# Seven block products for pairs of chunks at the end of a fused attention and feed-forward kernel, and zero products in planned pauses

## The chip, the cores and the metric

The kernel runs on one core of a Trainium2 chip. Each core has a matrix engine (PE, with its weight loads listed apart as PEld), a vector engine (DVE), a scalar engine (ACT), a general engine (POOL) and a queue engine that issues transfers (SP). They work at the same time and wait for one another by semaphores. The metric is the device time of one execution in microseconds (us); the median of several runs is compared.

## The reference

A linear attention is computed for 8 batches of 8 heads with 576 tokens and a head width of 64; its result, laid out as 4608 tokens by 512, goes through a feed-forward layer without bias.

```python
def phi(x):
    proj = np.einsum('bhsd,df->bhsf', x, w_phi)
    proj = proj - np.max(np.abs(proj), axis=-1, keepdims=True)
    return np.concatenate([np.exp(proj), np.exp(-proj)], axis=-1)
q_p, k_p = phi(q), phi(k)
kv = np.einsum('bhsf,bhsd->bhfd', k_p, v)
z = np.sum(k_p, axis=2)
num = np.einsum('bhsf,bhfd->bhsd', q_p, kv)
den = np.einsum('bhsf,bhf->bhs', q_p, z)[..., None] + 1e-06
x = (num / den)          # as 4608 x 512
h = x @ w_in             # 512 x 2048
r = np.maximum(h, 0.0)
out = (r * r) @ w_out    # 2048 x 512
```

## The kernel before

**Attention.** The 64 heads are handled as 32 pairs of heads (`p`). The first six pairs go through `early`, the others through `visit` (L847) and `late` (L936). One visit is a block of PE work: it starts the keys of pair i+1 (L588) and the queries of pair i (L856), forms keys times values of pair i (L644, L649) and the numerators of pair i-1 (L876). `late` holds what DVE, ACT and POOL do for a pair between two visits: maxima over partitions, two exponentials, the denominators. `tokens` then divides and writes the result of a pair into a ring of fp16 pairs (high part and remainder, L829 and L832), which holds six chunks of 256 tokens; its second half, `ring1`, is allocated when the weights are ready.

**Feed-forward.** `moe(c, f, w_done)` handles chunk `c` (18 chunks of 256 tokens) and block `f` (8 blocks of 256 hidden columns): 144 groups in all. `gemm1` (L1026) multiplies 4 slices of 128 of the 512 inputs, for each of two halves of 128 columns, in three products of fp16 parts (high by high, high by low, low by high): 24 matmuls of 256 columns into the PSUM tile `ph`. ACT applies Relu (L1035) and squares twice (L1039, L1041), DVE takes the remainder `gl` (L306), and `gemm2` (L1058) multiplies the squares by the output weights, again in three products: 12 matmuls of 512 columns into two `po` tiles, which gather over the 8 blocks and are then scaled and stored (`store`, L1076 and L1087).

**Order.** All work is entered in a planner (`P.add`) with an assumed duration, the operations that it follows, the tiles that it uses, and a rank. `order` runs a list scheduler over five queues by these numbers and the instructions are issued in the order that comes out, so each engine's order is fixed before the program runs. An operation of a lower rank goes first; on PE an operation of another array mode must be lower by `STAY` = 6. Pair `p` has ranks around 4.5 p, a visit i has rank 4.5 i + 1.3, and group n = 8 c + f of the feed-forward has rank `LEAD` + n = 36 + n. Its evictions have ranks lower by 1000, so they go ahead of all else on their engines. Ranks between -50 and 70 are replaced by a table found by an earlier search (`RANKS`, read by `improve`).

**PSUM.** The attention holds the tiles `pp` (two banks), `pn`, `pv` and `pz`; the feed-forward holds `ph` (one bank) and `po` (two). The four attention tiles have one buffer each, and their users are chained one after another.

**Start.** Eight products of zeros (`warm`, L419) run before the first load has landed. The weights are loaded, split in two parts and scaled by powers of two (`power`, with the tops `TOP_W` and `TOP_X`) beside the first six pairs.

Of the kernel before, what the change touches and what calls it, by code (L numbers as in the profile page):

```python
# [247 lines left out]
class Tiles:  # L248
# [10 lines left out]
    def __getitem__(self, n):  # L259
# [33 lines left out]
def tile_kernel(ctx, tc, qp, kp, vp, w_phi, w_in, w_out, out):  # L293
# [711 lines left out]

    chunk_done = {}

    def moe(c, f, w_done):
        n = c * NFP + f
        m, bank = LEAD + n, n + BANKS  # L1010
        half, c0 = divmod(c * T % RING, HR)
        po = [("po", 2 * BANKS + 2 * c + i) for i in range(2)]

        after = list(w_done[f, True])
        if f == 0:
            for p in range(NPAIR):
                after += [o for t0, t1, o in ring_of[p] if t0 < c * T + T and t1 > c * T]

        def gemm1():
            ph = ph_[bank]  # L1020
            for j in range(2):
                ff = 2 * f + j
                k = 0
                for t in range(KT):
                    for (w, x) in ((0, 0), (0, 1), (1, 0)):
                        PE.matmul(out=ph[:, j, :], lhsT=win[w][:, t, 128 * ff:128 * ff + 128],  # L1026
                                  rhs=ring[half][x][:, t, c0:c0 + T], start=k == 0, stop=k == 3 * KT - 1)
# [7 lines left out]
        o = P.add("ACT", act_us(512, 1), lambda: A.activation(  # L1035
            out=r_[n], in_=ph_[bank], func=AF.Relu, scale=cw[:, f, 0:1]), [g1], [("ph", bank), ("r", n)], Q,
                  other=[("DVE", 0.70, lambda: V.tensor_scalar(out=r_[n], in0=ph_[bank], scalar1=cw[:, f, 0:1], scalar2=0.0,
                                                               op0=ALU.mult, op1=ALU.max), None)])
        sq = P.add("ACT", act_us(512), lambda: A.activation(out=gh_[n], in_=r_[n], func=AF.Square),  # L1039
                   [o], [("r", n), ("gh", n)], Q)  # L1040
        o = P.add("ACT", act_us(512), lambda: A.activation(out=r_[n], in_=r_[n], func=AF.Square),  # L1041
                  [sq], [("r", n)], Q, other=[("DVE", 0.70, lambda: V.tensor_tensor(
                      out=r_[n], in0=r_[n], in1=r_[n], op=ALU.mult), 4.0)])
        o = P.add("DVE", 0.70, lambda: sub(V, gl_[n], r_[n], gh_[n].bitcast(F32)),
                  [o, sq], [("r", n), ("gh", n), ("gl", n)], Q, lock=4.0)


        def gemm2():
            upper = lambda x: x.bitcast(BF16).rearrange("p j (c w) -> p j c w", w=2)[:, :, :, 1]
            low, near = wout[f][1:]  # L1050
            parts = [(s, i) for s in range(3) for i in range(2)]
            if n == NCH * NFP - 1:
                parts = [(s, i) for i in range(2) for s in range(3)]
            for s, i in parts:
                g, w = ((gh_[n], highs[f]), (upper(gh_[n]), low), (gl_[n], near))[s]
                for j in range(2):
                    ff = 2 * f + j
                    PE.matmul(out=po_[po[i][1]], lhsT=g[:, j, 128 * i:128 * i + 128], rhs=w[:, j, :],  # L1058
                              start=(ff == 0 and s == 0), stop=(ff == 2 * NFP - 1 and s == 2))

        g2 = P.add("PE", 2.69, gemm2, [o] + list(w_done[f, False]),
                   [("gh", n), ("gl", n)] + po, m + 1.5)
        if f:
            g2.after.append(last2[0])
        last2[0] = g2
        if f == NFP - 1:
            for i in range(2):
                store(c, i, po[i], g2, Q)

    def store(c, i, po, g2, Q):  # L1070
        tt = 2 * c + i
# [11 lines left out]
        for E, x in ways:  # L1083
            n = x.stop - x.start
            o = P.add(*(("DVE", dve_us(n) + 0.11) if E is V else ("ACT", out_us(n) + 0.09)), lambda E=E, x=x: scaled(E, x),
                      [g2] + [scales] * (E is A), [po, ("o", tt)], Q)
            P.add("SP", 0.38, lambda x=x: SP.dma_start(out[128 * tt:128 * tt + 128, x], o_[tt][:, x]), [o], [("o", tt)], Q,  # L1087
                  land=1.8, xfer=0.7)

    last2 = [None]  # L1090

# [31 lines left out]
    for p in range(NPAIR):  # L1123
# [8 lines left out]
        if p == EARLY:  # L1132
# [5 lines left out]
    last_cc = cc[:, 2 * NCH - 2:2 * NCH]  # L1138
    scales = P.add("DVE", 0.2, lambda: V.tensor_tensor(out=cc2, in0=last_cc, in1=last_cc, op=ALU.mult),
                   [scale_of[B - 1]], [], PER_PAIR * NPAIR, lock=4.0)  # L1140
    for c in range(NCH):
        for f in range(NFP):
            moe(c, f, w_done)
    pool_next.after += pool_prep
    for op in P.ops:
        op.after = [x for a in op.after for x in (chunk_done[a[1]] if isinstance(a, tuple) else [a])]
    P.close()
    with tc.manual_schedule():
        for op in P.improve():
# [29 lines left out]


# [31 lines left out]
```

## Time and profile before

| | |
|---|---|
| median of 3 runs | 1044.22 us (1042.35 to 1044.98) |
| the profiled execution | 1042.14 us |
| its span, first to last instruction | 1040.4 us |
| PE busy | 1021.0 us, 98% |
| DVE busy | 735.0 us, 71% |
| ACT busy | 639.6 us, 61% |
| POOL busy | 169.0 us, 16% |
| mean granted PE clock | 0.998 |

The busy time of PE contains the overlap of pipelined matmuls, so it doesn't tell by itself how much of it is needed. The span has a start in which transfers and the preparation of weights go on, a long middle in which visits and feed-forward groups alternate, and an end with feed-forward groups alone.

### The profile page before, as it was taken

The page shows a single profiled execution, that of the slowest core. Times are in us where ns is not written, and L with a number is a line of the kernel's source. Part 1 is how long each engine was busy: PE and PEld are TensorE (multiplying, and loading weights), DVE is VectorE, ACT ScalarE, POOL GpSimd, SP SyncE. Part 2 cuts the span into 40 slices and gives each one's busy share as a digit, 9 for nine tenths or more (in the row PEclk, how much of TensorE's full clock was granted, in tenths as well). Part 3 has the DMA queues.
Part 4 walks back from the last instruction along what each step waited for, and adds up shares of the span by engine and source line. Part 5 has one row for each costly group of instructions (what it writes and reads, how often), then busy time and mean ns, then how long its engine had stood idle before and what let it go on. Part 6 is the DMA issues. An engine that isn't in the chain of part 4 may idle for free.

```text
span 1040.4 us, 19694 instructions
## 1 busy us (share of the span) xinstructions
PE 1021.0 (98%) x7874; PEld 701.0 (67%) x7874; DVE 735.0 (71%) x1525; ACT 639.6 (61%) x1118; POOL 169.0 (16%) x87
## 2 busy tenths in 40 slices
PE   8879999999999999999999999999999999999998
PEld 6546676676666766766766766676766666777775
DVE  6889788998877888889778787778787845111111
ACT  7988786667656666676666666566665635333333
POOL 2334231111111111121011111101111101000000
PEclk9999999999999999999999999999999999999999
DMA  9744322222212222222121221211121101000000
GB/s 358 271 158 140 134 67 58 79 58 58 78 59 78 58 65 67 79 61 76 31 65 47 76 60 58 73 28 57 45 66 34 44 17 38 1 22 21 1 21 21
DMA packets 66144, 73.49 MB, mean 71 GB/s; under 512 B 35204, under 2 KB 44036, under 8 KB 64004
## 3 DMA queue, kind: packets, MB, share of 16 engines
q1 hardware_dynamic: 66052, 72.22, 21.7%
q8 instruction: 62, 1.02, 0.4%
q14 instruction: 30, 0.25, 0.1%
HBM read 59.18 MB, written 12.99 MB: 69 GB/s over the span
## 4 chain that ended last, share of the span: by engine, by line
PE 94%; ACT 2%; DMA 2%; DVE 1%; SPq 0%; issue 0%; ACTq 0%
PE po L1058 37%; PE ph L1026 36%; PE pz L644 4%; PE pn L876 3%; PE pn L856 3%; PE pp L588 2%; PE pv L876 2%; DMA k<-in_kp_dram 2%; PE pz L649 1%; PE pz L864 1%; PE pv L644 1%; PE pz L594 1%; PE pn L758 0%; PE pn L775 0%; PE pp L739 0%; PE pv L677 0%
## 5 line engine op out<-in xcount | busy, mean ns | idle before, releaser
L1026 PE MATMUL ph<-ring,win 128*128 128x256 f16 x3456 | 401.0, 273 | 0.0
L1026 PEld LDWEIGHTS <-win 128*128 128x128 f16 x3456 | 336.6, 98 | 71.7 <-issue 6.7
L1035 ACT ACTIVATE r<-ph,cw 128x512 f32<-128x512 f32 x144 | 98.9, 687 | 262.1 <-PE ph L1026 261.1
L306 DVE TENSOR_TENSOR gl<-r,gh 128x512 bf16<-128x512 f32 x144 | 102.2, 709 | 193.7 <-ACT r L1041 192.9
L960 POOL PARTITION_ALL_REDUCE mx<-pt x52 | 119.8, 2303 | 604.2 <-ACT pt L310 557.5
L1058 PE MATMUL po<-wh,gh 128*128 128x512 f32 x576 | 170.3, 416 | 0.0
L1058 PE MATMUL po<-wl,gh 128*128 128x512 bf16 x576 | 149.6, 382 | 0.0
L1058 PE MATMUL po<-wl,gl 128*128 128x512 bf16 x576 | 148.0, 379 | 0.0
L1058 PEld LDWEIGHTS po<-wh,gh 128*128 128x128 f32 x576 | 97.8, 189 | 19.8 <-issue 4.7
L1058 PEld LDWEIGHTS <-gl 128*128 128x128 bf16 x576 | 56.3, 98 | 68.0
L1039 ACT ACTIVATE gh<-r 128x512 fp32r<-128x512 f32 x144 | 90.7, 630 | 6.8 <-PE po L1058 2.4
L1058 PEld LDWEIGHTS <-gh 128*128 128x128 bf16 x576 | 44.7, 98 | 73.3 <-issue 39.7
L1041 ACT ACTIVATE r<-r 128x512 f32<-128x512 f32 x144 | 90.7, 630 | 4.6
L610 ACT ACTIVATE e<-e 128x512 f32<-128x512 f32 x64 | 40.0, 626 | 35.7 <-DVE e L607 35.5
L604 DVE TENSOR_REDUCE km<-pp 128x4 f32<-128x512 f32 x54 | 36.6, 684 | 30.1 <-PE pp L588 30.0
L626 DVE TENSOR_TENSOR ez<-e 128x512 f32<-128x512 f32 x52 | 45.8, 880 | 5.1 <-ACT e L612 4.6
L644 PE MATMUL pz<-e,v 128*64 128x256 f32 x416 | 49.3, 379 | 0.0
L306 DVE TENSOR_TENSOR qe<-pt,mx 128x576 f32<-128x576 f32 x52 | 39.2, 753 | 10.0 <-POOL mx L960 9.8
L974 DVE SCALAR_TENSOR_TENSOR pt<-qe,zc,pt 128x576 f32<-128x576 f32 x52 | 41.7, 815 | 5.7 <-ACT pt L972 5.0
L972 ACT ACTIVATE pt<-qe,zc 128x576 f32<-128x576 f32 x52 | 40.1, 774 | 4.4 <-ACT qe L967 0.4
L612 ACT ACTIVATE e<-e 128x512 f32<-128x512 f32 x64 | 40.2, 628 | 1.4
L978 DVE STREAM_TRANSPOSE yt<-pt 128x576 f32<-128x576 f32 x52 | 40.3, 774 | 0.8
(205 smaller groups left out, 1257.2 us busy)
## 6 DMA issues: line engine op xcount, KB each, us to landing
v<-in_vp_dram SPq DMA_DIRECT2D x32, 320.0 KB
k<-in_kp_dram SPq DMA_DIRECT2D x32, 288.0 KB
q<-in_qp_dram SPq DMA_DIRECT2D x32, 288.0 KB
rb<-rd SPq DMA_DIRECT2D x64, 144.0 KB
out_dram<-o SPq DMA_DIRECT2D x34, 256.0 KB
td<-kvs SPq DMA_DIRECT2D x26, 128.0 KB
kz<-td SPq DMA_DIRECT2D x104, 32.0 KB
raw0i<-in_w_in_dram SPq DMA_DIRECT2D x1, 1024.0 KB
```

What stands on the lines that cost most here:

```text
L306: eng.tensor_tensor(out=out_, in0=a, in1=b_, op=ALU.subtract)
L626: o = P.add("DVE", dve_us(512), lambda n=n: V.tensor_tensor(out=ez_[n].rearrange("p t x -> p (t x)"), in0=e_[n][:, 0:2].rearrange("p t s f ...
L644: PE.matmul(out=to[64 * h:64 * h + 64, 0:256], lhsT=v_[p][:, t, h, :], rhs=e_[2 * p + h][:, t].rearrange("p s f -> p (s f)"), start=t == 0 ...
L876: PE.matmul(out=to[64 * h:64 * h + 64, :], lhsT=kz_[n][:, 128 * s_ + 64 * h:128 * s_ + 64 * h + 64], rhs=qe_[2 * n + h].rearrange("p (s x) ...
L960: o = P.add("POOL", par_us(S), lambda n=n, h=h: G.partition_all_reduce(mx_[n], pt_[p][:, h, :], channels=128, reduce_op=bass_isa.ReduceOp. ...
L974: o = P.add("DVE", 0.82, lambda h=h, qe=qe, y=y: V.scalar_tensor_tensor(out=y(), in0=qe(1), scalar=zc_[p][:, 2 * h + 1:2 * h + 2], in1=y() ...
L978: o = P.add("DVE", dve_us(S), lambda n=n, y=y: V.transpose(yt_["y", n - 2 * EARLY], y()), [o], [("pt", p), ("yt", ("y", n - 2 * EARLY))], ...
L1026: PE.matmul(out=ph[:, j, :], lhsT=win[w][:, t, 128 * ff:128 * ff + 128], rhs=ring[half][x][:, t, c0:c0 + T], start=k == 0, stop=k == 3 * K ...
L1035: o = P.add("ACT", act_us(512, 1), lambda: A.activation(out=r_[n], in_=ph_[bank], func=AF.Relu, scale=cw[:, f, 0:1]), [g1], [("ph", bank), ...
L1039: sq = P.add("ACT", act_us(512), lambda: A.activation(out=gh_[n], in_=r_[n], func=AF.Square), [o], [("r", n), ("gh", n)], Q)
L1041: o = P.add("ACT", act_us(512), lambda: A.activation(out=r_[n], in_=r_[n], func=AF.Square), [sq], [("r", n)], Q, other=[("DVE", 0.70, lamb ...
L1058: PE.matmul(out=po_[po[i][1]], lhsT=g[:, j, 128 * i:128 * i + 128], rhs=w[:, j, :], start=(ff == 0 and s == 0), stop=(ff == 2 * NFP - 1 an ...
```

## The change

The last four chunks (14 to 17) are handled as two pairs of chunks. For a pair of chunks and one block `f`, the first product is seen as a 2 by 2 block product: the weights as two halves of the columns by two halves of the inputs, the tokens as two halves of the inputs by two chunks. Seven products of blocks (`product`, six matmuls of 256 columns each) take the place of eight, so a pair and a block take 42 matmuls in place of 48. They need sums of blocks. Those of the weights (`add_w`, once for each `f`) and of the tokens (`add_x`, twice for each pair of chunks) are formed beforehand, mostly on DVE, in the new single tile `tm`, split in two fp16 parts and kept in tiles that the attention has left. The products go to `pz`, `pp` and `ph`; four DVE operations and one copy combine them, and the values go on through Relu, squares and `gemm2` as before. The results of the second chunk of a pair gather in `pn` and `pv`. Since sums of four values must stay in fp16's range, the tops of the powers of two are 2^-12 in place of 2^-14.

The ranks of the feed-forward are spread by `STEP` = 1.09; the table `RANKS` is another one, found for these ranks. Last, the planned order is searched for pauses of PE of over 0.7 us before 125 us; where an attention tile of PSUM is free in the plan, products of zeros into it are put there, as many of 0.214 us as fill 0.6 of the pause.

```diff
-TOP_W = 2.0 ** -14
-TOP_X = 2.0 ** -14
+TOP_W = 2.0 ** -12
+TOP_X = 2.0 ** -12
+STEP = 1.09
+FILL_TO = 125.0
+PAIRED = 14
+TAIL = LEAD + (STEP - 1.0) * PAIRED * NFP
...
+    tm_ = tiles(None, "tm", [128, 1024], F32, 1)
...
     def moe(c, f, w_done):
         n = c * NFP + f
-        m, bank = LEAD + n, n + BANKS
+        m, bank = LEAD + STEP * n, n + BANKS
...
+    def combine(fill, sums, use, halves, after, rank):
+        n = len(parts_w) + len(parts_x)
+        tm = lambda: tm_[n]
+        o = P.add("DVE", 1.3, fill, after + [ring1] + exps[NPAIR - 2], [("tm", n)], rank, lock=4.0)
+        o = P.add("DVE", 1.7, sums, [o], [("tm", n)], rank, lock=4.0)
+        hi = P.add("ACT", 1.06, lambda: A.activation(out=halves(0), in_=tm(), func=AF.Copy), [o], [("tm", n)] + use, rank,
+                   other=[("DVE", 0.64, lambda: V.tensor_copy(out=halves(0), in_=tm()), 4.0)])
+        return P.add("DVE", 1.28, lambda: sub(V, halves(1), tm(), halves(0)), [hi], [("tm", n)] + use, rank, lock=4.0)
...
+    def add_w(f, rank):
...
+            V.tensor_tensor(out=tm_[n].rearrange("p (t c) -> p t c", t=KT), in0=win[0][:, :, cs], in1=win[1][:, :, cs], op=ALU.add)
...
+            V.tensor_tensor(out=a22, in0=a21, in1=a22, op=ALU.add)
+            sub(V, a21, a11, a21)
+            sub(V, a11, a22, a11)
+            sub(V, a12, a12, a11)
...
+    def pair(c, f):
+        n = c * NFP + 2 * f
+        m = TAIL + n
+        Q = m - 1000.0
...
+        def product(to, l, r_):
+            fl, *al = left[l]
+            fr, *ar = right[r_]
+            n = 0
+            for k in range(2):
+                for x, y in ((0, 0), (0, 1), (1, 0)):
+                    PE.matmul(out=to, lhsT=fl(x, *al)(k), rhs=fr(y, *ar)(k), start=n == 0, stop=n == 5)
+                    n += 1
...
+        after = list(w_done[f, True]) + [w_ready] + x_ready + in_pair.get("pe", [])
+        if f == 0:
+            after += ready(c) + ready(c + 1)
+        reads = w_use + x_use
+        p1 = P.add("PE", 1.97, one, after, [px, pu] + reads, m)
+        p2 = P.add("PE", 2.62, two, [p1], [px, py] + reads, m + 0.01)
...
+        first, other = copy(T, lambda: r()[:, 2, :], lambda: pz_["w", g][:, 0:T])
+        o = P.add(*first, [p1] + old, [pu, rt], Q, other=[other])
+        u = P.add("DVE", dve_us(512), lambda: plus(r()[:, 0:2, :], X(0), wide(r()[:, 2, :])), [o], [px, rt], Q)
+        v = P.add("DVE", dve_us(512), lambda: plus(W(), X(1), wide(r()[:, 1, :])), [p2, u], [px, uv, rt], Q)
+        c22 = P.add("DVE", dve_us(T), lambda: plus(r()[:, 3, :], X(1)[:, 1, :], W()[:, 0, :]), [v], [px, uv, rt], Q)
+        c2 = P.add("DVE", dve_us(512), lambda: plus(r()[:, 1:3, :], Y(), W()), [v], [py, uv, rt], Q)
+        c3 = [P.add("ACT", act_us(512, 1), lambda i=i: A.activation(
+            out=r()[:, 2 * i:2 * i + 2, :], in_=r()[:, 2 * i:2 * i + 2, :], func=AF.Relu, scale=cw[:, f, 0:1]),
+            [c2, c22], [rt], Q + 0.1 * i) for i in range(2)]
+        for i in range(2):
+            done.append(squares(n + i, lambda i=i: r()[:, 2 * i:2 * i + 2, :], [c3[i]], [rt], Q + 0.1 * i))
+            second(n + i, c + i, f, done[i], m + 2.5 + i, po[i])
...
-    for c in range(NCH):
+    for c in range(PAIRED):
         for f in range(NFP):
             moe(c, f, w_done)
...
+    for c in range(PAIRED, NCH, 2):
+        first = TAIL + c * NFP - (6.0 if c == PAIRED else 8.0)
+        for f in range(3 if c == PAIRED else 0):
+            add_w(f, first + 0.5 * f)
+        for i in range(2):
+            add_x(c, i, [next(keep), next(keep)], first + 2.0 + 0.5 * i)
+        for f in range(3, NFP if c == PAIRED else 0):
+            add_w(f, first + 0.5 + f)
+        for f in range(NFP):
+            pair(c, f)
...
+    def zeros(tag, n, count):
+        to = {"pp": pp_, "pn": pn_, "pv": pv_, "pz": pz_}[tag]["fill", n]
+        for _ in range(count):
+            PE.matmul(out=to[:, 0, :] if tag == "pp" else to, lhsT=warmer[:, 0:128], rhs=warmer, start=True, stop=True)
...
+        if op.eng == "PE":
+            if last and last.end < FILL_TO and op.start - last.end > 0.7:
+                gaps.append((last.end, op.start))
+            last = op
+    fills = []
+    for n, (t0, t1) in enumerate(gaps):
+        free = [tag for tag in ("pp", "pv", "pz", "pn")
+                if all(y + 0.2 <= t0 or x >= t1 for (k, _), (x, y) in held.items() if k == tag)]
+        if free:
+            fills.append((t0, len(P.ops), lambda tag=free[0], n=n, count=int(0.6 * (t1 - t0) / 0.214): zeros(tag, n, count)))
```

More of the change, by code (lines that the diff above doesn't have):

```diff
@@ L264, in __getitem__, with shaped @@
         return self.made[n]
+    def shaped(self, n, shape, dtype):
+        assert n not in self.made and (self.first is None or n == self.first + len(self.made)), (self.tag, n)
+        self.made[n] = self.pool.tile(shape, dtype, name=f"{self.tag}_{len(self.made)}", tag=self.tag, bufs=self.n)
+        return self.made[n]
 def act_us(n, pointers=0):
@@ L1006, in tile_kernel, with ready, at_ring @@
     chunk_done = {}
+    def ready(c, rows=range(NP)):
+        return [o for p in range(NPAIR) if p % NP in rows for t0, t1, o in ring_of[p] if t0 < c * T + T and t1 > c * T]
+    def at_ring(c, x, rows):
+        half, c0 = divmod(c * T % RING, HR)
+        return ring[half][x][:, rows, c0:c0 + T]
     def moe(c, f, w_done):
         n = c * NFP + f
-        m, bank = LEAD + n, n + BANKS
-        half, c0 = divmod(c * T % RING, HR)
-        po = [("po", 2 * BANKS + 2 * c + i) for i in range(2)]
+        m, bank = LEAD + STEP * n, n + BANKS
         after = list(w_done[f, True])
         if f == 0:
-            for p in range(NPAIR):
-                after += [o for t0, t1, o in ring_of[p] if t0 < c * T + T and t1 > c * T]
+            after += ready(c)
         def gemm1():
@@ L1026, in gemm1 @@
                         PE.matmul(out=ph[:, j, :], lhsT=win[w][:, t, 128 * ff:128 * ff + 128],
-                                  rhs=ring[half][x][:, t, c0:c0 + T], start=k == 0, stop=k == 3 * KT - 1)
+                                  rhs=at_ring(c, x, t), start=k == 0, stop=k == 3 * KT - 1)
                         k += 1
@@ L1038, in moe, with squares, second @@
                                                                op0=ALU.mult, op1=ALU.max), None)])
[L1039 to L1045, printed above, removed]
+        g = squares(n, lambda: r_[n], [o], [("r", n)], Q)
+        second(n, c, f, g, m + 1.5, [("po", 2 * BANKS + 2 * c + i) for i in range(2)])
+    def squares(n, r, after, use, Q):
+        sq = P.add("ACT", act_us(512), lambda: A.activation(out=gh_[n], in_=r(), func=AF.Square),
+                   after, use + [("gh", n)], Q)
+        o = P.add("ACT", act_us(512), lambda: A.activation(out=r(), in_=r(), func=AF.Square),
+                  [sq], use, Q, other=[("DVE", 0.70, lambda: V.tensor_tensor(
+                      out=r(), in0=r(), in1=r(), op=ALU.mult), 4.0)])
+        return P.add("DVE", 0.70, lambda: sub(V, gl_[n], r(), gh_[n].bitcast(F32)),
+                     [o, sq], use + [("gh", n), ("gl", n)], Q, lock=4.0)
+    def second(n, c, f, g, rank, po):
+        bank = lambda i: {"po": po_, "pn": pn_, "pv": pv_}[po[i][0]][po[i][1]]
         def gemm2():
@@ L1051, in gemm2 @@
             parts = [(s, i) for s in range(3) for i in range(2)]
-            if n == NCH * NFP - 1:
+            if c >= NCH - 2 and f == NFP - 1:
                 parts = [(s, i) for i in range(2) for s in range(3)]
             for s, i in parts:
-                g, w = ((gh_[n], highs[f]), (upper(gh_[n]), low), (gl_[n], near))[s]
+                x, w = ((gh_[n], highs[f]), (upper(gh_[n]), low), (gl_[n], near))[s]
                 for j in range(2):
                     ff = 2 * f + j
-                    PE.matmul(out=po_[po[i][1]], lhsT=g[:, j, 128 * i:128 * i + 128], rhs=w[:, j, :],
+                    PE.matmul(out=bank(i), lhsT=x[:, j, 128 * i:128 * i + 128], rhs=w[:, j, :],
                               start=(ff == 0 and s == 0), stop=(ff == 2 * NFP - 1 and s == 2))
-        g2 = P.add("PE", 2.69, gemm2, [o] + list(w_done[f, False]),
-                   [("gh", n), ("gl", n)] + po, m + 1.5)
-        if f:
+        g2 = P.add("PE", 2.69, gemm2, [g] + list(w_done[f, False]), [("gh", n), ("gl", n)] + po, rank)
+        if last2[0]:
             g2.after.append(last2[0])
@@ L1085, in store, with take @@
             o = P.add(*(("DVE", dve_us(n) + 0.11) if E is V else ("ACT", out_us(n) + 0.09)), lambda E=E, x=x: scaled(E, x),
-                      [g2] + [scales] * (E is A), [po, ("o", tt)], Q)
+                      [g2] + [scales] * (E is A), [use, ("o", tt)], Q)
             P.add("SP", 0.38, lambda x=x: SP.dma_start(out[128 * tt:128 * tt + 128, x], o_[tt][:, x]), [o], [("o", tt)], Q,
                   land=1.8, xfer=0.7)
+    parts_w, parts_x, in_pair = {}, {}, {}
+    def take(use, shape, dtype, box):
+        if use not in box:
+            box[use] = {"e": e_, "qe": qe_, "pt": pt_, "mx": mx_, "n": n_, "rb": rb_, "v": v_, "k": k_, "q": q_, "r": r_}[use[0]].shaped(
+                use[1], shape, dtype)
+        return box[use]
@@ new lines, in add_x, with fill, sums @@
+    def add_x(c, rows, use, rank):
+        n = len(parts_w) + len(parts_x)
+        box = {}
+        halves = lambda x: take(use[x], [128, 1024], F16, box)
+        grid = lambda x: x.rearrange("p (h c t) -> p h c t", h=2, c=2)
+        def fill():
+            for i in range(2):
+                V.tensor_tensor(out=grid(tm_[n])[:, :, i, :], in0=at_ring(c + i, 0, slice(rows, KT, 2)),
+                                in1=at_ring(c + i, 1, slice(rows, KT, 2)), op=ALU.add)
+        def sums():
+            x = grid(tm_[n])
+            b11, b12, b21, b22 = x[:, 0, 0, :], x[:, 0, 1, :], x[:, 1, 0, :], x[:, 1, 1, :]
+            sub(V, b11, b12, b11)
+            sub(V, b12, b22, b12)
+            sub(V, b22, b22, b11)
+            sub(V, b21, b21, b22)
+        o = combine(fill, sums, use, halves, [o for i in range(2) for o in ready(c + i, (rows, rows + 2))], rank)
+        parts_x[c, rows] = o, use, lambda x, h, i: grid(halves(x))[:, h, i, :]
@@ L1147, in tile_kernel @@
     P.close()
+    def zeros(tag, n, count):
+        to = {"pp": pp_, "pn": pn_, "pv": pv_, "pz": pz_}[tag]["fill", n]
+        for _ in range(count):
+            PE.matmul(out=to[:, 0, :] if tag == "pp" else to, lhsT=warmer[:, 0:128], rhs=warmer, start=True, stop=True)
+    order = P.improve()
+    held, gaps, last = {}, [], None
+    for op in order:
+        for key in op.uses:
+            if key[0] in P.single:
+                x = held.setdefault(key, [op.start, 0.0])
+                x[1] = max(x[1], op.there)
+        if op.eng == "PE":
+            if last and last.end < FILL_TO and op.start - last.end > 0.7:
+                gaps.append((last.end, op.start))
+            last = op
@@ L1148, in tile_kernel @@
+    fills = []
[4 more added lines that the diff above has]
+            fills.append((t0, len(P.ops), lambda tag=free[0], n=n, count=int(0.6 * (t1 - t0) / 0.214): zeros(tag, n, count)))
     with tc.manual_schedule():
-        for op in P.improve():
-            op.fn()
+        for _, _, fn in sorted([(op.start, op.n, op.fn) for op in order] + fills, key=lambda x: x[:2]):
+            fn()
```

116 lines of the change are left out of this document (89 added, 27 removed).

## The prediction

> **What bounds the kernel now.** I read the page's busy shares first, then the chain that ended last, then the windows by stage, then the timeline of the end.
>
> ```profile
> span 1040.4 us, 19694 instructions
> ...
> PE 1021.0 (98%) x7874; PEld 701.0 (67%) x7874; DVE 735.0 (71%) x1525; ACT 639.6 (61%) x1118; POOL 169.0 (16%) x87
> ...
> DVE  6889788998877888889778787778787845111111
> ...
> PE 94%; ACT 2%; DMA 2%; DVE 1%; SPq 0%; issue 0%; ACTq 0%
> ```
>
> 94% of the chain is PE, so the end moves when PE's work does. DVE's row shows full slices up to about 0.8 of the span and ones after: the end is poor in DVE work. The windows (busy us of PE, PEld, DVE, ACT, POOL; granted clock; share of the DMA engines; GB/s) show where PE pauses:
>
> ```profile
> 0.00:26.00 26.00, 22.48 (x237) 15.60 (x238) 15.86 (x40) 18.22 (x35) 7.11 (x11) 0.93 0.93 358
> 26.00:52.00 26.00, 21.20 (x286) 14.19 (x286) 22.03 (x39) 23.70 (x44) 9.69 (x8) 1.00 0.76 272
> 52.00:78.00 26.00, 20.73 (x220) 13.02 (x218) 22.27 (x40) 22.19 (x44) 8.85 (x5) 1.00 0.49 158
> 78.00:104.00 26.00, 23.94 (x241) 16.98 (x238) 23.51 (x33) 22.60 (x37) 11.59 (x6) 1.00 0.41 140
> ...
> 104.00:840.00 736.00, 736.00 (x5560) 505.15 (x5559) 604.45 (x1298) 476.10 (x843) 126.80 (x56) 1.00 0.21 62
> 840.00:1040.00 200.00, 196.65 (x1340) 136.02 (x1338) 46.92 (x80) 76.78 (x122) 4.93 (x2) 1.00 0.06 18
> ```
>
> The first 104 us leave PE idle for 3.52 + 4.80 + 5.27 + 2.06 = 15.65 us. From 104 us on it has no pause but the last 3.35 us, in which the last block is scaled and stored. DVE is busy for 604.45 of 736 us in the middle (82%) and for 23% at the end.
>
> **The products saved.** The chain in order of time gives a group's price, the timeline its period at the end:
>
> ```profile
> 337.74 2.62 PE ph L1026 x24
> 340.37 2.67 PE po L1058 x12
> ```
>
> ```profile
> 885.58 2.78 PE L1026 MATMUL ph<-ring,win 128*128 128x256 f16 x24
> ...
> 1023.21 2.78 PE L1026 MATMUL ph<-ring,win 128*128 128x256 f16 x24
> ...
> 1025.75 1.18 PE L1058 MATMUL po<-wh,gh 128*128 128x512 f32 x4
> ...
> 1028.50 2.78 PE L1026 MATMUL ph<-ring,win 128*128 128x256 f16 x24
> ```
>
> A group takes 2.62 + 2.67 = 5.29 us, and starts follow one another by 1028.50 - 1023.21 = 5.29 us too: no slack. One matmul of 256 columns costs 2.62 / 24 = 0.109 us by the chain, or (1025.75 - 1023.21) / 24 = 0.106 us by starts. Two pairs of chunks with 8 blocks make 16 pairs with 6 matmuls less each: 96 matmuls, 10.2 to 10.5 us. I take 10.3. The new products have the same shapes and a fresh weight load for each, as now.
>
> A busy PE alone doesn't prove that its slots are needed. [...]
>
> **The work that replaces them.** Prices of DVE and ACT by shape (busy, mean ns of one):
>
> ```profile
> L306 DVE TENSOR_TENSOR gl<-r,gh 128x512 bf16<-128x512 f32 x144 | 102.2, 709 | 193.7 <-ACT r L1041 192.9
> L607 DVE TENSOR_TENSOR e<-pp,km 128x512 f32<-128x512 f32 x54 | 36.4, 677 | 1.2 <-PE pz L644 0.4
> L631 DVE TENSOR_TENSOR es<-ez 128x256 f32<-128x256 f32 x52 | 24.0, 462 | 0.7
> L466 DVE SCALAR_TENSOR_TENSOR u<-u,raw0i 128x1024 int32<-128x1024 int32 x1 | 1.2, 1216 | 0.0
> L1035 ACT ACTIVATE r<-ph,cw 128x512 f32<-128x512 f32 x144 | 98.9, 687 | 262.1 <-PE ph L1026 261.1
> L1041 ACT ACTIVATE r<-r 128x512 f32<-128x512 f32 x144 | 90.7, 630 | 4.6
> L530 ACT ACTIVATE win<-u,cw 128x1024 f16<-128x1024 f32 x7 | 7.9, 1142 | 2.8 <-DVE cw L412 2.8
> L310 ACT ACTIVATE n<-pv 128x256 f32<-128x256 f32 x26 | 9.8, 379 | 2.9 <-PE pv L876 2.8
> ```
>
> A pair and a block take PE 42 x 0.107 + 2 x 2.67 = 9.83 us. DVE needs three combinations at 0.68, one at 0.46 and two remainders at 0.71: 3.92 us. ACT needs a copy of 0.38, two Relu at 0.69 and four squares at 0.63: 4.28 us. Both are under half of PE's time. In order: after the second half of the products PE has the two `gemm2` of the pair before, 5.34 us. Within it v, c22 and c2 must leave `pp`, `pz` and `ph` (0.68 + 0.46 + 0.68 = 1.82 us). An addition already running on DVE delays them by 1.85 us at most (four of 0.46 in one planned step): 3.7 of 5.34 us, so nothing waits. [...] I take 0, with 0 to 0.5.
>
> Sums: twelve of them. One is 1.22 (filling) + 4 x 0.46 + 1.14 (ACT) + 1.22 = 5.4 us, in series because `tm` has one buffer; 4.3 us of it is DVE's, 51 us in all. The end has the DVE time for it (below 31 of 166 us are busy), so their cost is zero as long as they are early enough:
>
> ```profile
> 870.00:1036.00 166.00, 166.00 (x1120) 115.49 (x1119) 30.97 (x51) 61.81 (x97) 0.00 (x0) 1.00 0.04 14
> ```
>
> **The seam.** The first pair needs what the attention leaves: its PSUM tiles and the ring of batch 7. Today the last visits lie so:
>
> ```profile
> 851.27 0.69 PE L856 MATMUL pn<-q,wraw 64*128 64x512 f32 x1
> ...
> 856.82 1.38 PE L1026 MATMUL ph<-ring,win 128*128 128x256 f16 x11
> ```
>
> ```profile
> 880.71 1.30 PE L876 MATMUL pn<-qe,kz 128*64 128x320 f32 x8
> ...
> 885.07 0.82 DVE L832 SCALAR_TENSOR_TENSOR ring<-rb,cb,ring 128x576 f16<-128x576 f32 x1 [0.84 <-ACT ring L829]
> ```
>
> After 880.71 come (1028.50 - 885.58) / 5.29 + 1 = 28 groups, so 116 were begun before the last visit, and 111 before the one at 851.27. Plain groups now end at 112. Were the attention no faster, PE would run dry. It should be: the visit before the last has rank 4.5 x 31 + 1.3 = 140.8, and the feed-forward stood at 36 + 111 = 147, 6 more, which is `STAY`. So visits are held back by rank, not by data. With the same lead the group there is n = (147 - 36) / 1.09 = 102, and five groups later 107 at the last visit. That leaves 5 x 5.29 = 26 us. The ring is complete 885.89 - 880.71 = 5.2 us after the last visit begins, and the sum that needs it takes 5.4: 11 us, or 22 if two others are still in `tm` before it. So there is no pause, with 4 to 15 us to spare; each group short beyond that costs 5.3 us. For nine fewer groups beside it, DVE in the middle rises: (604 - 9 x 0.71) / (736 - 9 x 5.29) = 87%. That such a density runs without stall is shown here:
>
> ```profile
> 182.00:234.00 52.00, 52.00 (x400) 35.83 (x398) 48.17 (x104) 33.15 (x60) 9.43 (x4) 1.00 0.23 68
> ```
>
> 93% of DVE beside a full PE. I take 0, with 0 to 10 us. The steps between visits in this stretch are the shortest that data allow so far, 25.3 us:
>
> ```profile
> 185.53 0.69 PE L856 MATMUL pn<-q,wraw 64*128 64x512 f32 x1
> ...
> 210.79 0.69 PE L856 MATMUL pn<-q,wraw 64*128 64x512 f32 x1
> ```
>
> With 4.5 / 1.09 groups for a visit the new step would be 6.6 (the PE work of a visit: 856.82 - 851.27 and some 1.0 for the keys of the next pair) + 4.13 x 5.29 = 28.4 us, so there is room.
>
> **Zeros, and the start.** The only loss of clock is this, in windows of PE alone:
>
> ```profile
> 8.00:10.00 2.00, 0.31 (x4) 0.95 1.06 434
> 10.00:12.00 2.00, 2.00 (x18) 0.50 0.97 397
> 12.00:14.00 2.00, 2.00 (x16) 0.70 1.09 447
> ```
>
> and the keys of one pair in the timeline, then and later:
>
> ```profile
> 9.79 2.17 PE L588 MATMUL po<-wraw,k 64*128 64x128 f32 x16 [1.69 <-DMA k<-in_kp_dram]
> ...
> 35.38 1.16 PE L588 MATMUL po<-wraw,k 64*128 64x128 f32 x16
> ```
>
> It is (0.05 + 0.50 + 0.30) x 2 = 1.7 us; the keys of one pair took 2.17 us there and 1.16 later. This bounds what zeros can bring, and since PE isn't full there, only part would reach the end: I take 0.8. [...] Their price: 15.65 us of pauses, filled to 0.6, is at most 9 us of PE work; where an input comes earlier than planned, zeros stand in front of it, and a `pp` or `pz` not yet read makes PE wait. In pauses of under 2 us I cost that at 0, with 0 to 4. The new table of ranks moves every instruction of the first 70 ranks, loads on SP too. It can't win more than the 15.65 us of pauses; a share of it either way is my bound, -5 to +5, value 0, since nothing in the profile says which. The new tops change values only.
>
> **Sum.** 1042.1 - 10.3 - 0.8 = 1031.0 us for the profiled execution, which ran 2.1 below the median; against the median 1044.2 - 11.1 = 1033.1 us.
>
> **Rivals.**
> - *The seam pauses.* If the attention drifts by two to four groups, PE waits 3 to 10 us before the first pair: 1036 to 1043. For it: the step needed, 28.4 us, is only 3 above the shortest shown. Against: 11 of 26 us are needed.
> - *The attention doesn't get faster (slower than before).* If DVE, not rank, sets the visits' pace, the last visit still begins after what were 116 groups. Only 112 exist: 4 x 5.3 = 21 us of pause, and 11 us for the ring and the sum: 1033 + 32 = 1065. It gives the gain away from two groups later than 110 on, and makes the kernel slower by more than noise beyond. For it: the 93% above. Against: the lead of just 6 ranks.
> - *The start changes.* Better ranks: 1026 to 1030. Worse, or zeros in the way: 1036 to 1042.
> - *Nothing is saved.* If products now overlap something that sets the pace (hand-overs, weight loads), the 96 matmuls turn into waits: 1044. Against: the equal periods.
>
> **How the numbers follow.** A difference of about 0.3% (3.1 us) is what can be told from none. Forecast, 1030 to 1036: 0.58. Better start: 0.12. Seam pause: 0.12, half of it within 0.3%. Worse start: 0.07, mostly still faster. Nothing saved: 0.04. Slow attention: 0.07. Faster: 0.58 + 0.12 + 0.06 + 0.05 = 0.81; same 0.12; slower 0.07. The range from 1026 to 1041 leaves out the slow attention, nothing saved and some of the pauses.
>
> **What would show it.** At the end a pair's products and its two `gemm2` should repeat every 9.8 to 9.9 us, 0.64 less than 2 x 5.29, PE without a pause; a longer period breaks the first term. About 107 plain groups should be begun at the last visit, and the first product of a pair should follow a `gemm2` at once. The clock should read 1.00 from 8 to 14 us, and PE's idle time before 104 us should be near 15.65 us less the zeros. PE waiting for DVE in the middle, or a wait on the sums, makes the prediction wrong.

## The result and the profile after

The changed kernel takes 1032.61 us (median of 4 runs, 1030.94 to 1035.78); the kernel before took 1044.60 us beside it (1042.35 to 1045.76). The ratio is 0.9891, with a 95% interval from 0.9870 to 0.9911: 12.0 us faster. The prediction was 1033.1 us. The profiled execution happens to be the slowest of the four, 1035.78 us with a span of 1034.0 us, so against the profile before (span 1040.4 us) only 6.4 us are to be found between the two traces.

The page of the changed kernel, with the lines that answer to those of before:

```profile
span 1034.0 us, 19633 instructions
...
PE 1011.2 (98%) x7722; PEld 695.1 (67%) x7805; DVE 818.5 (79%) x1663; ACT 653.5 (63%) x1147; POOL 170.0 (16%) x88
...
DVE  6879687898888887898889888888888897954433
...
PE 94%; DVE 2%; ACT 2%; issue 1%; DMA 1%; SPq 0%; DVEq 0%; ACTq 0%
```

PE still carries 94% of the chain. DVE has 83.5 us more to do, and its row shows where: the slices at the end that held ones now hold fours and threes. The windows of the changed kernel for the start, the middle, the stretch between the last visit and the first pair, and the pairs (busy us of PE, PEld, DVE, ACT, POOL; clock; DMA share; GB/s):

```profile
0.00:26.00 26.00, 21.77 (x238) 13.77 (x239) 15.70 (x37) 17.47 (x33) 6.41 (x11) 1.00 0.92 355
26.00:52.00 26.00, 22.38 (x293) 15.72 (x290) 22.19 (x39) 22.23 (x43) 11.89 (x9) 1.00 0.74 263
52.00:78.00 26.00, 21.58 (x211) 12.98 (x209) 19.89 (x31) 20.07 (x39) 10.61 (x6) 0.93 0.46 157
78.00:104.00 26.00, 24.73 (x242) 16.38 (x242) 23.92 (x40) 23.34 (x41) 10.06 (x5) 1.00 0.45 152
...
104.00:831.00 727.00, 723.17 (x5457) 498.60 (x5512) 617.68 (x1325) 478.16 (x848) 131.02 (x58) 1.00 0.21 63
831.00:868.00 37.00, 36.72 (x246) 25.18 (x249) 30.20 (x54) 19.29 (x30) 0.00 (x0) 1.00 0.07 23
868.00:1030.00 162.00, 160.88 (x1054) 112.47 (x1068) 88.38 (x140) 72.39 (x118) 0.00 (x0) 1.00 0.04 14
```

From 104 us on no wait of PE is listed; the 0.5% missing from full go with matmul records that the trace lost: 7722 matmuls stand beside 7805 weight loads, and 7805 is what 7874 of before less 96 products plus 27 zeros makes. DVE is busy for 617.68 / 727 = 85% of the middle, where 87% was worked out, and for 55% of the time of the pairs.

The gain has two parts, the start and the rest. The first feed-forward group of the changed kernel starts here,

```profile
94.52 2.79 PE L1040 MATMUL ph<-ring,win 128*128 128x256 f16 x24
```

while before it started at 90.72 us. From that start to the end of the span are 1034.0 - 94.5 = 939.5 us, against 1040.4 - 90.7 = 949.7 us before. So the part with the products gives 10.2 us, and this execution lost 3.8 us at the start against the profile before.

The pairs repeat like this at the end, in the timeline of PE:

```profile
994.65 0.82 PE L1221 MATMUL pz<-ring,win 128*128 128x256 f16 x6
1004.59 0.82 PE L1221 MATMUL pz<-ring,win 128*128 128x256 f16 x6
1014.51 0.82 PE L1221 MATMUL pz<-ring,win 128*128 128x256 f16 x6
```

A pair and a block take 9.92 to 9.94 us: 0.64 to 0.66 less than two plain groups of 5.29. Sixteen of them save 10.2 to 10.6 us.

### The profile page after: what moved, and what is told of

It reads as the page before. It is cut to its first block, busy times and chain, and to the rows that moved or that the text cites. A ratio compares the mean times of both kernels' runs of the same rounds, so it can differ in the third digit from the quotient of the medians.

```text
span 1034.0 us, 19633 instructions
## 1 busy us (share of the span) xinstructions
PE 1011.2 (98%) x7722; PEld 695.1 (67%) x7805; DVE 818.5 (79%) x1663; ACT 653.5 (63%) x1147; POOL 170.0 (16%) x88
## 4 chain that ended last, share of the span: by engine, by line
PE 94%; DVE 2%; ACT 2%; issue 1%; DMA 1%; SPq 0%; DVEq 0%; ACTq 0%
PE po L1078 33%; PE ph L1040 29%; PE pz L654 4%; PE pp L1221 4%; PE pn L886 3%; PE pn L866 3%; PE pp L598 2%; PE pv L886 2%; PE ph L1221 2%; PE pn L1078 2%; PE pv L1078 2%; PE pz L659 1%; PE pz L1221 1%; PE pz L874 1%; PE pv L654 1%
## 5 line engine op out<-in xcount | busy, mean ns | idle before, releaser
L1040 PE MATMUL ph<-ring,win 128*128 128x256 f16 x2688 | 311.9, 273 | 0.0
L1040 PEld LDWEIGHTS <-win 128*128 128x128 f16 x2688 | 261.5, 98 | 55.7 <-issue 6.6
L1049 ACT ACTIVATE r<-ph,cw 128x512 f32<-128x512 f32 x112 | 76.8, 686 | 148.7 <-PE ph L1040 148.3
L315 DVE TENSOR_TENSOR gl<-r,gh 128x512 bf16<-128x512 f32 x112 | 79.4, 709 | 65.3 <-ACT r L1059 64.6
L1078 PE MATMUL po<-wl,gh 128*128 128x512 bf16 x436 | 117.0, 381 | 5.1
L1057 ACT ACTIVATE gh<-r 128x512 fp32r<-128x512 f32 x112 | 70.6, 630 | 3.6
L1059 ACT ACTIVATE r<-r 128x512 f32<-128x512 f32 x112 | 70.6, 630 | 3.6
L1253 ACT ACTIVATE qe<-qe,cw 128x512 f32<-128x512 f32 x32 | 22.8, 714 | 62.0 <-DVE qe L1236 62.0
L620 ACT ACTIVATE e<-e 128x512 f32<-128x512 f32 x64 | 39.9, 624 | 31.3 <-DVE e L617 31.1
L315 DVE TENSOR_TENSOR gl<-qe,gh 128x512 bf16<-128x512 f32 x32 | 22.1, 691 | 39.6 <-ACT qe L1059 38.4
```

What stands on the lines that cost most here:

```text
L315: eng.tensor_tensor(out=out_, in0=a, in1=b_, op=ALU.subtract)
L1049: o = P.add("ACT", act_us(512, 1), lambda: A.activation(out=r_[n], in_=ph_[bank], func=AF.Relu, scale=cw[:, f, 0:1]), [g1], [("ph", bank), ...
L1059: o = P.add("ACT", act_us(512), lambda: A.activation(out=r(), in_=r(), func=AF.Square), [sq], use, Q, other=[("DVE", 0.70, lambda: V.tenso ...
L1078: PE.matmul(out=bank(i), lhsT=x[:, j, 128 * i:128 * i + 128], rhs=w[:, j, :], start=(ff == 0 and s == 0), stop=(ff == 2 * NFP - 1 and s == 2))
```

## The experiments

All were run beside the kernel before, which took 1045.1 to 1045.4 us in these comparisons. A table of them all comes first: the median, the ratio to the kernel before with its interval, and from each profile the start of the first feed-forward group and the time from there to the end of the span.

| kernel | median us | ratio (95%) | first group at | from there to the end |
|---|---|---|---|---|
| before | 1045.1 to 1045.4 | 1 | 90.72 | 949.7 |
| whole_change | 1033.75 | 0.9886 (0.9868 to 0.9904) | 92.50 | 939.5 |
| no_pairs | 1042.32 | 0.9976 (0.9961 to 0.9991) | 91.93 | 949.5 |
| no_zeros | 1035.24 | 0.9905 (0.9887 to 0.9923) | 92.74 | 939.5 |
| old_start | 1034.38 | 0.9900 (0.9877 to 0.9922) | 92.74 | 939.5 |
| zeros_alone | 1045.87 | 1.0001 (0.9989 to 1.0012) | 96.25 | 949.7 |
| old_start_zeros | 1035.78 | 0.9904 (0.9884 to 0.9925) | 93.83 | 939.5 |
| fewer_zeros | 1034.42 | 0.9891 (0.9867 to 0.9915) | 91.59 | 939.5 |
| old_start_two | 1035.75 | 0.9910 (0.9884 to 0.9936) | 94.49 | 939.5 |
| seam_near | 1044.66 | 0.9997 (0.9982 to 1.0012) | 91.54 | 950.9 |
| three_pairs | 1085.44 | 1.0373 (1.0351 to 1.0396) | 93.09 | 991.0 |

The last two columns come from one profile of each kernel. The last one takes two values, whatever the table of ranks and the zeros: 949.5 to 949.7 us without the pairs and 939.5 us with them, but for the last two kernels, which pause. All other differences lie ahead of the first group.

**The change again.**

> The changed kernel again, as the yardstick for the runs beside it. Both theories: 1031 to 1035 us, 10 to 13 us below the kernel before. A profile with the clock at 1.00 all through should start its first feed-forward group at about 93 us (94.5 in the first profile, which lost about 1.7 us of clock at 73 us).

It came to 1033.75 us, and its first group started at 92.50 us, as expected of a clock at 1.00.

**The pairs taken away.**

```diff
-PAIRED = 14
+PAIRED = 18
```

> PAIRED = 18, so all 144 groups are plain ones; the new ranks, the spread of 1.09 and the zeros stay. Theory (the gain is PE work taken out at the end): 16 x 0.64 = 10.3 us above the changed kernel, 1042 to 1044. Rival (the gain comes from the new order of the start, the products being hidden anyway): no more than 3 us above the changed kernel.

Measured: 1042.32 us, 8.6 us above whole_change. The rival (the gain sits in the start) falls. The new tops and the spread ranks are still in this kernel, so they don't make the 10 us. Between the profiles the price is 949.5 - 939.5 = 10.0 us. The medians lie closer than that; this kernel had its clock at 0.999 or 1.00 in 9 of 12 runs, whole_change at 0.998 or 0.999 in its four. Against the kernel before, 2.8 us remain for the new ranks and the zeros together, with an interval of the ratio that just excludes none.

**The zeros taken away.**

```diff
-for _, _, fn in sorted([(op.start, op.n, op.fn) for op in order] + fills, key=lambda x: x[:2]):
+for _, _, fn in sorted([(op.start, op.n, op.fn) for op in order], key=lambda x: x[:2]):
```

> The changed kernel without the 27 zero products in the pauses. Theory (zeros only keep the clock, and PE isn't the bound at the start): 0 to 1.7 us above the changed kernel, with a granted clock below 1 for some 3 us in the first 104 us. Rival (zeros stand in front of work whose input has come): 1 to 4 us faster than the changed kernel.

Measured: 1035.24 us, 1.5 above whole_change, inside the 0 to 1.7 of the theory. The two sets of runs don't overlap (1033.98 to 1037.97 against 1032.76 to 1033.87), but the intervals of the ratios do, and the first four runs of the changed kernel (1030.94 to 1035.78) overlap with these too. The windows of 2 us (busy us of PE; clock; DMA share; GB/s) show clock that was lost here, at two places; whole_change read 1.00 in all such windows up to 104 us:

```profile
34.00:36.00 2.00, 0.99 (x8) 0.81 1.04 415
36.00:38.00 2.00, 2.00 (x24) 0.50 1.00 391
38.00:40.00 2.00, 2.00 (x22) 0.84 1.00 314
72.00:74.00 2.00, 1.69 (x14) 0.69 0.46 149
74.00:76.00 2.00, 2.00 (x19) 0.50 0.00 0
76.00:78.00 2.00, 1.19 (x10) 0.95 0.16 31
```

That is (0.19 + 0.50 + 0.16 + 0.31 + 0.50 + 0.05) x 2 = 3.4 us of clock. Yet in this profile the first group starts at 92.74 us, only 0.24 later than with full clock. Either lost clock is not lost time at the start, or the 27 zeros cost about what the clock lost here is worth; these two profiles can't tell which.

**The pairs with the old table of ranks.**

```diff
-m, bank = LEAD + STEP * n, n + BANKS
+m, bank = LEAD + min(n, 34) + LATE * max(0, n - 34), n + BANKS    # LATE = 1.1292, RANKS of before, no zeros
```

> The pairs with the old table of ranks: groups 0 to 34 keep the old rank 36 + n, from there on the ranks are spread by 1.129 so that the first pair has the same rank as in the changed kernel; no zeros. Theory (products give 10.3 us, the start nothing): 1033 to 1035 us, 10 us below the kernel before, and the start as before (first feed-forward group at 90.7 us). Rival (the new table carries part of the gain): 1035 to 1038.

Measured: 1034.38 us, 10.7 below the kernel before, inside the theory's range. The new table of ranks isn't what makes the kernel faster: without zeros, the old one (1034.38) does as well as the new (1035.24). The first group did not start at 90.7 us, as I expected, but at 92.74. This execution lost 3.4 us of clock before 20 us, the profile before 1.7; that this makes the 2.0 us was not shown.

**Zeros in the kernel before.**

```diff
+    order = P.improve()
...
+            fills.append((t0, len(P.ops), lambda tag=free[0], n=n, count=int(0.6 * (t1 - t0) / 0.214): zeros(tag, n, count)))
```

> The kernel before with zeros put into its planned pauses by the same rule, nothing else. Theory (zeros are worth the clock that is lost at the start: over the 17 runs of the kernel before, 0.998 of the clock goes with about 1042.9 us and 0.993 with 1047.3): clock 0.998 or more in nearly all runs, 1042 to 1043 us, 2 to 3 us below the kernel before, with less spread. Rival (zeros are hidden, the chip differs by itself): same spread of clock and times as the kernel before.

Measured: 1045.87 us against 1045.38, ratio 1.0001. The theory falls, and so does its rival, for the clock did get better: 0.998 or more in 10 of 12 runs, where 3 of 23 of the kernel before had that. At the same clock the kernel with zeros is slower: at 0.998 these runs took 1045.3 to 1047.0 us, the kernel before 1041.6 to 1044.2. So the zeros cost about as much as the better clock gave.

**Zeros with the pairs and the old table.**

> The pairs with the old table of ranks, and zeros. Theory (products 10.3 us and zeros 1.5 to 3 us add up, the new table gives nothing): 1031.5 to 1033.5 us, as the changed kernel or below it, clock 0.998 or more. Rival (the new table itself is worth something): over 1034 us.

Measured: 1035.78 us, 1.4 above old_start without zeros, though the ratios' intervals overlap. The gain forecast for zeros does not add to that of the products. The number is what the rival forecast (over 1034 us), but old_start speaks against its reason, a worth of the new table by itself. The timeline of PE shows what one group of zeros does here, between the queries and the numerators:

```profile
56.82 0.38 PE L716 MATMUL pz<-wraw,q 64*128 64x128 f32 x2
57.13 1.90 PE L1337 MATMUL pv<-o 128*128 128x512 bf16 x8
59.09 1.19 PE L769 MATMUL pv<-qe,kz 128*64 128x288 f32 x8
```

In the kernel before the same numerators follow the queries at once:

```profile
56.37 0.38 PE L705 MATMUL pz<-wraw,q 64*128 64x128 f32 x2
56.69 1.19 PE L758 MATMUL pv<-qe,kz 128*64 128x288 f32 x8
```

The plan had a pause there, the chip has none: the pause came before the queries, where PE waited 1.52 us for DVE in both. The eight zeros push the numerators back by 1.9 us. What the other places of zeros cost is not shown.

**Some of the zeros.**

```diff
-        if free:
+        if free and n != 4:     # fewer_zeros; old_start_two has: free and n < 2
```

> The changed kernel without the six zeros planned for the pause at 53.5 us; the other five places stay. With those six the pause of 1.5 us ahead of the queries at 56 us ended 1.0 us later than without any, and the clock never fell at that place. Theory (each place of zeros is worth the clock it keeps less the work it pushes back): 1032.5 to 1033.5 us, 0 to 1 us below the changed kernel. Rival (zeros are free wherever they are): no difference, or slower by the clock that now falls at 55 us.

> The pairs with the old table of ranks and zeros in the first two planned pauses only (before 10 us). All zeros together cost this table 1.4 us (1035.8 against 1034.4), and eight of them at 57 us stood for 1.9 us ahead of matmuls that could have run. Theory (the cost comes from the later places, the gain from the clock kept early): 1032 to 1034 us with a clock of 0.998 or more. Rival (the clock lost before 20 us is hidden behind the loads, so keeping it brings nothing): 1034 to 1035 us, as without zeros.

Measured: 1034.42 us (0.7 above whole_change) and 1035.75 us (1.4 above old_start). Both miss the theory. For fewer_zeros the rival holds (no difference: the ratios are 0.9891 and 0.9886). For old_start_two the rival is nearer, and the clock was not kept either: 0.993 to 0.997, where 0.998 or more was expected. In its profile the clock of the first 104 us was 0.97, some 3 us of clock lost, though zeros stand in the pauses before 10 us. Sizes of 1 us at the start are below what these runs resolve.

**The first pair brought nearer to the attention's end.**

```diff
-m, bank = LEAD + STEP * n, n + BANKS
+m, bank = LEAD + STEP * min(n, 32) + LATE * max(0, n - 32), n + BANKS    # LATE = 1.0
-TAIL = LEAD + (STEP - 1.0) * PAIRED * NFP
+TAIL = LEAD + STEP * 32 + LATE * (PAIRED * NFP - 32) - PAIRED * NFP
```

> The changed kernel with ranks spread by 1.09 for the first 32 groups only and by 1.0 after, which brings the first pair 7.2 ranks nearer to the attention's end. Theory (the plain groups left at the last visit cover the ring and the sums; at 106 groups there are 6, 13 us more than needed): visits are held by rank, so the last one now comes near group 112 or after it, the cover is gone, and PE pauses for 10 to 16 us ahead of the first pair: 1043 to 1049 us. Rival (the attention is held by its data and runs as fast as before): no pause, 1032 to 1035 us.

Measured: 1044.66 us, 10.9 above whole_change; the whole gain is gone, as the theory had it. All 112 plain groups were begun before the last visit, at 862.93 us, and only the last `gemm2` stands between it and the first pair. Then the products wait for sums (the brackets give the idle time before them and what ended it):

```profile
862.93 1.30 PE L887 MATMUL pn<-qe,kz 128*64 128x320 f32 x8
...
867.80 0.82 PE L1222 MATMUL pz<-ring,win 128*128 128x256 f16 x6
...
871.77 0.38 PE L1222 MATMUL pp<-k,e 128*128 128x256 f16 x2 [2.39 <-DVE k L316]
876.03 0.37 PE L1222 MATMUL pp<-q,e 128*128 128x256 f16 x1 [3.88 <-ACT q L1123]
877.29 0.58 PE L1222 MATMUL pp<-q,e 128*128 128x256 f16 x2 [0.89 <-DVE q L316]
...
884.52 0.83 PE L1222 MATMUL pp<-ring,win 128*128 128x256 f16 x6 [1.96 <-DVE qe L1237]
```

The four pauses make 9.1 us, and the time from the first group to the end is 950.9 - 939.5 = 11.4 us longer. The clock of 0.91 in the 39 us from 861 us on would be 3.5 us of clock, part of it within the pauses. The rival (the attention is held by its data and keeps its pace) falls for these ranks, as the queries of the visits show:

```profile
590.70 0.69 PE L867 MATMUL pn<-q,wraw 64*128 64x512 f32 x1
...
836.11 0.69 PE L867 MATMUL pn<-q,wraw 64*128 64x512 f32 x1
```

Between these two lie eight steps of 30.7 us, where the visits of the changed kernel follow one another by 27.0 us on average. A rank step of 4.5 groups asks 6.6 + 4.5 x 5.29 = 30.4.

**Three pairs of chunks.**

```diff
-PAIRED = 14
+PAIRED = 12
-m, bank = LEAD + STEP * n, n + BANKS
+m, bank = LEAD + STEP * min(n, 32) + LATE * max(0, n - 32), n + BANKS    # LATE = 1.352, TAIL as above
```

> The last six chunks as three pairs, ranks spread by 1.352 from group 32 on, so that the last visit should come near group 91 of 96. 8 more pairs and blocks save 8 x 0.64 = 5.1 us. Theory (DVE holds the attention's pace: 24.2 us of step asked, 23.7 us of DVE work in it): visits fall back to steps of 25 to 26 us, 3 to 5 groups are short at the seam, a pause of 10 to 25 us, 1037 to 1053 us. Rival (there is room in the attention): no pause, 1027 to 1029 us.

Measured: 1085.44 us, well over the theory's range; the direction is right, its size wrong. The 96th plain group starts before 765 us; the two visits that follow find no groups between them, and PE stands still. In the windows of three_pairs:

```profile
752.00:778.00 26.00, 22.84 (x187) 14.35 (x184) 22.57 (x50) 13.51 (x24) 4.91 (x2) 1.00 0.19 54
778.00:804.00 26.00, 12.79 (x62) 6.04 (x64) 24.94 (x59) 10.97 (x21) 6.86 (x3) 0.64 0.09 23
804.00:830.00 26.00, 8.68 (x34) 4.10 (x31) 22.52 (x40) 9.65 (x15) 3.04 (x1) 0.57 0.12 34
830.00:856.00 26.00, 16.16 (x109) 11.68 (x109) 22.12 (x36) 10.70 (x16) 0.00 (x0) 0.74 0.00 0
```

PE is idle for 3.16 + 13.21 + 17.32 + 9.84 = 43.5 us, at a clock down to 0.57, with DVE at 85 to 96%. Its longest waits there are for copies of the attention by ACT into `pt` (4.89 and 10.30 us) and for a token sum of the first pair (12.62 us). The step that I assumed for the visits, 25 to 26 us, was too short: while groups lasted, the visits of this kernel came in seven steps of 26.9 us:

```profile
566.85 0.69 PE L867 MATMUL pn<-q,wraw 64*128 64x512 f32 x1
...
755.32 0.69 PE L867 MATMUL pn<-q,wraw 64*128 64x512 f32 x1
```

Single steps among these go from 25.2 to 30.9 us, so a short step seen once is not the pace. The same pace, 27.0 us, is that of the changed kernel: its 26 visits lie between 135.07 and 809.95 us. With ranks spread by 1.09 or by 1.352 it is the same, so here it is not rank that sets it. It need not be the chip either: the order on each engine is fixed before the run, PE was busy for all of 560 to 755 us without a wait, and a full PE walks through visits and groups at the pace of that order. So the limit is that of the data as the plan assumes them; whether the chip could deliver them faster was not tried (DVE was at 84 to 86% in two windows of that stretch).

## Why the prediction held

**What bounds the kernel.** PE, as read. The 96 removed matmuls, 10.2 to 10.5 us by their price, brought 10.0 to 10.2 us from the first group to the end in all three comparisons with and without pairs: no_pairs with whole_change, the kernel before with old_start, zeros_alone with old_start_zeros.

**The products: 10.3 us predicted, 10.0 to 10.2 measured** from the first group to the end. A pair and a block took 9.92 to 9.94 us. The prediction has two figures for this that don't fit together: 9.83, with 0.107 us a matmul, and 0.64 less than 2 x 5.29, which is 9.94 and lies above its own sign of 9.8 to 9.9. By 0.107 a plain group would take 24 x 0.107 + 2.67 = 5.24, not 5.29. The saving was right, and the period of 9.83 too short. Between the starts at 1004.59 and 1014.51 the products took 4.51 us, where 4.49 was worked out, and the two `gemm2` 5.41, where it was 5.34 (their first matmul starts at 1009.10). The doubt in the prediction, slack behind a busy PE, did not apply: the weight loads' share was 67% before and after, and the removed matmuls came off in full but for 0.5 us at most.

**The replacing work at nothing.** Held. One repeat of the last block in the timeline of the changed kernel:

```profile
1018.78 0.69 DVE L1236 TENSOR_TENSOR ez<-pp,qe 128x512 f32<-128x512 f32 x1
...
1022.65 0.69 DVE L315 TENSOR_TENSOR gl<-qe,gh 128x512 bf16<-128x512 f32 x1 [2.11 <-ACT qe L1059]
...
1024.27 0.82 PE L1078 MATMUL po<-wh,gh 128*128 128x512 f32 x2
```

From v (1018.78) to the remainder's end (1023.34) it took 4.56 us, where the prices from before add up to 1.82 + 0.69 + 1.26 + 0.71 = 4.48 us: 0.08 us is left for all the hand-overs. The range of 0 to 0.5 us in the forecast was my estimate for such hand-overs; no run shows that term. PE used the value 0.9 us later. Also, v didn't have to wait for all of the second half, only for its part in `pp`: it starts at 1018.78 us, while the products run to 1019.02. So the chain of the last pair has a margin of 0.9 us.

**The seam.** Predicted: 102 groups begun at the visit before the last, 107 at the last, 4 to 15 us to spare. In the changed kernel:

```profile
831.57 1.30 PE L886 MATMUL pn<-qe,kz 128*64 128x320 f32 x8
...
836.43 2.78 PE L1040 MATMUL ph<-ring,win 128*128 128x256 f16 x24
...
862.90 2.78 PE L1040 MATMUL ph<-ring,win 128*128 128x256 f16 x24
...
868.19 0.82 PE L1221 MATMUL pz<-ring,win 128*128 128x256 f16 x6
```

After the last visit come (862.90 - 836.43) / 5.29 + 1 = 6 plain groups, so 106 were begun; at the visit before, at 809.95 us, it was 103. The last sum that the first pair needs ends on DVE here, 13 us before the pair:

```profile
853.94 1.22 DVE L315 TENSOR_TENSOR q<-tm,q 128x1024 f16<-128x1024 f32 x1 [0.52 <-ACT q L1122]
```

One sum took 5.5 us (849.68, the start of its filling, to 855.16), where 5.4 was worked out. The number was right, its reason only half so, and in part by luck: the prediction had the visits held back by rank, with a step of 28.4 us in the changed kernel. They came by 27.0. (Nor was 25.3 us the shortest step of the kernel before: from 162.89 to 185.53 us it took 22.6.) seam_near shows that rank holds them when it is spread by 1.0, three_pairs that at 27.0 us a step more spread brings nothing, because the planned order has reached what its assumed data allow.

**Zeros and start: 0.8 us for the zeros, 0 for the ranks.** The zeros measured 1.5 us with the new table, 0 in the kernel before and -1.4 with the old table and the pairs: not one value, and none clear of its interval. Both ends, 1.7 us of clock and zeros in front of ready work (1.9 us in old_start_zeros), were seen. The new ranks are within 1 us of the old ones without zeros, as taken; with zeros the new table is 2.0 us faster (1033.75 against 1035.78), with intervals that overlap. Only ranks and zeros together, 2.8 us in no_pairs, are just clear of none.

**What was forecast to be seen** at the start held in part. PE's idle time before 104 us was 4.23 + 3.62 + 4.42 + 1.27 = 13.5 us, where 15.65 less 27 zeros of 0.214 us, as planned, would be 9.9 (three zeros took 0.81 us at 87.69, one alone 0.38: 0.22 from start to start): the zeros were not simply taken out of the idle time. The clock was 1.00 at 8 to 14 us, but fell later, to 0.50 at 74 to 76 us, after a pause of 1.35 us that no zeros filled:

```profile
73.76 1.42 PE L749 MATMUL pp<-ident,pt 128*128 128x128 f32 x6 [1.35 <-ACT qe L760]
75.11 2.15 PE L785 MATMUL pn<-qe,kz 128*32 128x288 f32 x16
```

## What to carry to other kernels

Where the period of a repeated group equals the sum of its own work on one engine, as here, taking work off that engine paid almost one for one (10.0 to 10.2 us of 10.2 to 10.5), and engines with about half their time free (DVE busy for 55% of the time of the pairs, ACT for 45%) carried what replaces it. The condition lies at the seam: the replacing work needs tiles, data and sums that an earlier stage must release in time, and each plain group that is missing in between is 5.29 us less cover, as much as eight pairs and blocks save. Fillers put into planned pauses are only as good as the plan: where the real pause lies elsewhere they stand in front of ready work, for 1.9 us at the place shown of old_start_zeros.

## What the runs showed of the hardware

**Runs differ by their start.** The time from the first feed-forward group on repeats to 0.2 us between the profiles of all kernels that have the same number of pairs and don't pause at the seam. The two profiles of the changed kernel start that group at 94.52 and 92.50 us. So what runs of one kernel differ by lies ahead of that group, as far as the profiles reach. In the kernel before the granted clock goes with it: over 23 runs 0.998 stands beside 1041.6 to 1044.2 us, and 0.992 to 0.993 beside 1046.4 to 1049.4.

**The clock can fall after a pause of 1.35 us, and often doesn't.** The changed kernel's windows after the pause of 1.35 us:

```profile
72.00:74.00 2.00, 0.65 (x6) 0.98 0.65 188
74.00:76.00 2.00, 2.00 (x14) 0.50 0.31 107
76.00:78.00 2.00, 2.00 (x19) 0.66 0.00 0
```

It lost (0.02 + 0.50 + 0.34) x 2 = 1.7 us, the same as in the kernel before at 9 to 14 us after a pause of 1.69 us: 3.4 us at a clock of 0.50. The windows of 2 us show six such drops that lost 1.7 us each (one in before, one in after, two in no_zeros, two in zeros_alone); a seventh, in old_start from 10 to 20 us, lasted twice as long and lost 3.4 us. The second profile of the same program (whole_change) went through the same pause with its clock at 1.00:

```profile
73.27 0.87 PE L749 MATMUL pp<-ident,pt 128*128 128x128 f32 x6 [1.35 <-ACT qe L760]
```

At this one place the clock fell in two profiles (after, no_zeros) and read 1.00 in three (whole_change, no_pairs, seam_near), and the kernel before kept its clock at 1.00 after pauses of 1.46 to 1.52 us (ended at 29, 35 and 55 us). So the length of one pause does not decide; what does is not shown.
